# Set attention and a maxout layer: pooling in column-tiled form, paced loads, and another order in the head

## The chip, the cores and the metric

The kernel runs on one core of a Trainium2 chip. The metric is the device time of one execution in microseconds (us). TensorE (PE) multiplies, VectorE (DVE) and ScalarE (ACT) take results out of the eight PSUM banks, GpSimd (POOL) issues loads and adds in on-chip memory, and SyncE (SP) issues output stores and transposing transfers.

## The reference

For each of four batches b, x[b] is 12544 x 128 and the 32 inducing points I are 32 x 128:

```python
def mab(q, kv):
    s = scale * (q @ kv.transpose(0, 2, 1))
    s = s - s.max(-1, keepdims=True)
    a = np.exp(s)
    a /= a.sum(-1, keepdims=True) + 1e-09
    return a @ kv
h = mab(I, x)          # pooling: 32 points look at all of x
a = mab(x, h)          # every row of x looks at the 32 points
h1 = a @ w1; h2 = a @ w2           # 128 -> 1024
out = np.maximum(h1, h2) @ w_out   # 1024 -> 128
```

So h of a batch needs the whole of that batch, and only then can rows of the output be made.

## The kernel before, in words

A batch is 98 chunks of 128 rows. A chunk holds every 98th row, so that a transfer is contiguous for each partition. x lives in on-chip memory twice: as loaded (tiles xn, seven or eight parts of up to 14 chunks, twelve slots that all batches share) and transposed (xT, one tile for even and one for odd batches). Batch 0 is transposed by PE in the head of the kernel (L233, L237, L240); batches 1 to 3 by transposing transfers that SP issues (L168).

Pooling of a part, before: p1_scores multiplies each chunk of xT by the inducing points, 14 products of 32 columns (L249), and ACT takes the exponential into et (L258). p1_accum multiplies each chunk of xn by et and sums 14 products in PSUM (L292). VectorE adds the result into hacc (L303), and GpSimd adds et into eacc (L305). At the end of a batch GpSimd folds eacc (small_fold, L310 and L311), small_h sums it over partitions with fp32 products by ones (L339), takes the reciprocal (L343) and makes hT, h transposed and repeated four times (L346). small_hwd makes h(w2 - w1) (L371), small_m1 makes h w1 w_out (L392).

The maxout is computed as max(h1, h2) = h1 + relu(h2 - h1). So a group of chunks needs: a stage (L479), the scores of four quarters of chunks against h in column-tiled form, with an exponential on ACT (L491) into e; phases (L827), four row-tiled products at a time, one for each quarter, each filling a PSUM bank that ACT (L843) or VectorE (L846) turns into relu; finals (L652), products of 128 columns by w_out that sum over the 1024 inner columns; dens (L519, L529) for the softmax denominators; and an eviction by VectorE (L692) that multiplies by the reciprocals, after which SP stores (L717). The part h1 goes in as a linear term, a product by m1, within a phase.

TensorE knows three modes here: full (one 128 x 128 array), row (four arrays of 32 rows) and col (four of 32 columns). Phases are in row mode, stages in col mode, the rest in full mode.

The order of instructions is fixed when the program is written out. A class Clock estimates when each engine and bank will be free, and a loop chooses at each step: a phase, if banks and data are expected ready; otherwise one final (final_one); a stage when the staged work runs low. side_work puts in the pooling of the next batch at due points that are counted in chunks done, and only when the modelled data are ready:

```python
p_first, p_step = (16, 5) if b == 1 else (0, 7)
for i in range(7):
    s = int(p_first + p_step * i)
    at(base + s, p1_scores, b, i)
    at(base + s + 2, p1_accum, b, i)
```

The engines run that order in their queues; each waits only for its operands and for buffers to come free. keep_busy puts products by zeros into waits that the model foresees (L630), and fill does so in the head (L537).

## Time and profile before

| | |
|---|---|
| time, median of 3 runs | 339.89 us (339.79 to 341.38) |
| profiled span | 337.8 us, TensorE clock granted 1.0 |
| DMA moved | 50.60 MB, mean 150 GB/s |
| HBM read, written | 27.80 MB, 25.69 MB |
| relu on ACT, L843 | 460 of 600 ns |
| relu on VectorE, L846 | 324 of 681 ns |
| finals on PE, L652 | 3136 |
| transposing transfers, L168 | 42, landing 3.4 us after issue |

The page names a group of instructions by its line in the code, its engine and operation, and the tiles written and read. A PE instruction's duration includes its way through the array, so that the sum of durations counts overlapping work twice; what a group of products takes from the next is the time between starts. In the first 28 us the kernel pools batch 0 as its parts arrive, and finals start at about 28.2 us. The pooling of batches 1 to 3 lies at about 46 to 82, 123 to 154 and 188 to 233 us, among phases and finals. The last 85 us and more have none.

### The profile page before, as it was taken

What the parts mean: (1) busy time and instruction counts of PE and PEld (TensorE: products, weight loads), DVE (VectorE), ACT (ScalarE), POOL (GpSimd) and SP (SyncE); (2) the same over time, 40 slices, a digit from 0 to 9 for tenths busy, and PEclk for the clock granted to TensorE, in tenths of its full rate; (3) what the DMA queues carried; (4) which work ended last, traced back from release to release, by engine and by line L of the source; (5) the groups of instructions that cost most, each with busy time, mean ns of one, the idle gap of its engine ahead of it and who ended that gap; (6) DMA issues with size and microseconds to landing.
All of it is one profiled execution on the core that took longest, in us unless ns stands there. A gap on an engine that the chain in (4) does not pass through costs nothing.

```text
span 337.8 us, 13042 instructions
## 1 busy us (share of the span) xinstructions
PE 329.2 (97%) x5636; PEld 255.4 (76%) x5636; DVE 286.8 (85%) x525; ACT 279.3 (83%) x532; POOL 45.5 (13%) x72
## 2 busy tenths in 40 slices
PE   7988999999999999999999999999999999999996
PEld 3876777777777777787777778877777777777785
DVE  2248999989988899998899989889999998898873
ACT  2558888896996998888998888887999899989961
POOL 7270002234000011144000012121000000000000
PEclk9999999999999999999999999999999999999999
DMA  7999989948985879529976679621222322231233
GB/s 127 212 255 213 199 206 183 177 133 168 244 225 156 174 144 190 135 95 177 249 211 127 156 168 201 147 78 67 103 86 97 109 95 74 88 125 66 95 126 111
DMA packets 60313, 50.60 MB, mean 150 GB/s; under 512 B 42304, under 2 KB 44768, under 8 KB 60256
## 3 DMA queue, kind: packets, MB, share of 16 engines
q1 hardware_dynamic: 54576, 35.35, 40.2%
q0 software_dynamic: 5680, 14.42, 22.0%
q8 instruction: 44, 0.72, 0.9%
q14 instruction: 13, 0.11, 0.1%
HBM read 27.80 MB, written 25.69 MB: 158 GB/s over the span
## 4 chain that ended last, share of the span: by engine, by line
PE 85%; POOL 1%; ACT 1%; DMA 1%; DVE 1%; issue 1%; SPq 0%; POOLq 0%
PE ps L652 56%; PE ps L827 21%; PE ps L479 2%; PE ps L249 2%; PE ps L292 2%; PE ps L339 1%; DMA xT<-xn 1%; PE ps L519 1%; POOL eacc L305 1%; DVE relu L846 1%; ACT relu L843 1%; POOL eacc L310 0%; PE ps L371 0%; SPq L168 0%; PE ps L630 0%
## 5 line engine op out<-in xcount | busy, mean ns | idle before, releaser
L843 ACT ACTIVATE relu<-ps 128x512 f16<-128x512 f32 x460 | 245.8, 600 | 38.2 <-PE ps L827 32.0
L846 DVE TENSOR_SCALAR relu<-ps 128x512 f16<-128x512 f32 x324 | 208.8, 681 | 20.9 <-PE ps L827 18.6
L652 PE MATMUL ps<-woutp,relu 128*128 128x128 f16 x3136 | 222.2, 220 | 0.0
L652 PEld LDWEIGHTS <-relu 128*128 128x128 f16 x3136 | 177.3, 98 | 38.4 <-issue 27.8
L827 PE MATMUL ps<-e,hwd 32*128 32x512 f16 (+2 forms) x880 | 88.6, 360 | 0.5 <-ACT e L491 0.3
L692 DVE TENSOR_TENSOR o<-ps,rp 128x512 f32<-128x512 f32 (+3 forms) x108 | 68.5, 634 | 8.3 <-PE ps L652 5.4
L827 PEld LDWEIGHTS <-hwd 32*128 32x128 f16 x880 | 24.9, 91 | 20.8 <-issue 1.1
L827 PE MATMUL ps<-m,e 32*128 32x128 f16 x381 | 38.6, 217 | 0.0
L305 POOL TENSOR_TENSOR eacc<-eacc,et 128x448 f32<-128x448 f32 x18 | 18.6, 1035 | 81.8 <-ACT et L258 81.8
L827 PEld LDWEIGHTS <-e 32*128 32x128 f16 x381 | 21.3, 92 | 2.9 <-issue 0.2
L258 ACT ACTIVATE et<-ps 128x448 f16<-128x448 f32 (+2 forms) x29 | 15.6, 538 | 3.0 <-PE ps L249 2.9
L249 PE MATMUL ps<-inducingT,xT 128*128 128x32 f16 x392 | 15.5, 177 | 1.3 <-DMA xT<-xn 0.5
L162 POOL DMA_DIRECT2D xn<-in_x_dram x29 | 15.7, 553 | 2.5 <-POOLq L960 0.8
L249 PEld LDWEIGHTS <-xT 128*128 128x128 f16 x392 | 13.1, 96 | 2.3 <-ACT xT L240 0.8
L300 POOL CAST eacc<-et 128x448 f32<-128x448 f16 x3 | 1.7, 556 | 89.9 <-ACT et L258 89.9
L237 DVE COPY xT<-ps 128x1024 f16<-128x1024 f16 (+2 forms) x8 | 5.1, 632 | 9.4 <-PE ps L233 9.4
L240 ACT COPY xT<-ps 128x768 f16<-128x768 f16 (+2 forms) x8 | 5.6, 704 | 8.9 <-PE ps L233 8.9
L491 ACT ACTIVATE e<-ps 128x512 f16<-128x512 f32 (+2 forms) x21 | 11.9, 571 | 0.0
L479 PE MATMUL ps<-xT,hT 128*32 128x512 f16 (+3 forms) x114 | 10.5, 366 | 0.1
L292 PE MATMUL ps<-et,xn 128*128 128x32 f16 x294 | 10.6, 176 | 0.0
L292 PEld LDWEIGHTS <-xn 128*128 128x128 f16 x294 | 9.7, 96 | 0.0
L233 PE MATMUL ps<-identity,xn 128*128 128x128 f16 x98 | 6.8, 219 | 0.5 <-DMA xn<-in_x_dram 0.4
(75 smaller groups left out, 100.2 us busy)
## 6 DMA issues: line engine op xcount, KB each, us to landing
out_dram<-o SPq DMA_DIRECT2D x90, 256.0 KB, 2.4
xn<-in_x_dram POOLq DMA_DIRECT2D x27, 448.0 KB, 11.2
out_dram<-o SPq DMA_DIRECT2D x10, 128.0 KB, 2.0
wf<-in_moe_w_dram POOLq DMA_DIRECT2D x4, 256.0 KB, 11.6
xT<-xn SPq DMA_TRANSPOSE x42, 3.4
out_dram<-o SPq DMA_DIRECT2D x6, 64.0 KB, 1.8
out_dram<-o SPq DMA_DIRECT2D x2, 192.0 KB, 3.2
xn<-in_x_dram POOLq DMA_DIRECT2D x1, 256.0 KB, 13.6
```

Source lines behind the costliest of these rows:

```text
L162: nc.gpsimd.dma_start(out=xn_at[b, i][:, 0:n, :], in_=xr[b, :, k0 : k0 + n, :])
L249: nc.tensor.matmul(out=ps[:, j * M : (j + 1) * M], lhsT=xT_tiles[b % 2][:, k0 + j, :], rhs=inducingT, start=True, stop=True,)
L258: nc.scalar.activation(out=et[:, 0:n, :], in_=ps[:, 0 : n * M], func=AF.Exp, scale=scale)
L292: nc.tensor.matmul(out=ps[:, 0:M], lhsT=xn[:, j, :], rhs=et[:, j, :], start=(j == 0), stop=(j == n - 1))
L305: nc.gpsimd.tensor_add(out=acc, in0=acc, in1=et)
L479: nc.tensor.matmul(out=ps[32 * q : 32 * (q + 1), 128 * t : 128 * (t + n)], lhsT=hq, rhs=xT[:, c : c + n, :], start=True, stop=True, tile_p ...
L491: nc.scalar.activation(out=blk.e2[:, 0 : 128 * wd], in_=ps[:, 0 : 128 * wd], func=AF.Exp, scale=st[0]["rs"] if blk.b == 0 else scale,)
L652: nc.tensor.matmul(out=g.ps[:, 128 * c : 128 * (c + 1)], lhsT=g.blk.relu[q][:, 128 * (jb * w4 + t) : 128 * (jb * w4 + t + 1)], rhs=woutp[: ...
L692: nc.vector.tensor_mul(osb[:, 0:n, :], g.ps[:, 0 : n * C].rearrange("p (s c) -> p s c", s=n), rp)
L827: nc.tensor.matmul(**seq[i])
L843: nc.scalar.activation(out=dst, in_=src, func=AF.Relu)
L846: nc.vector.tensor_scalar(out=dst, in0=src, scalar1=0.0, scalar2=None, op0=ALU.max)
```

## The change

Pooling of batches 1 to 3 is written anew, in units of 16 chunks (U), six to a batch (NU), with two chunks over (REST):

- pool_scores holds the inducing points as weights and streams xT through four column tiles, 512 columns each. ACT's exponential gives E, 32 points in each of four groups of partitions, and a running sum along its row (accum_out into es), so that GpSimd's adds go.
- E then has points on partitions, and the sum over x needs rows there; pool_turn has SP transpose E by a transfer. pool_accum multiplies in 16 column-tiled products of 128 columns, and VectorE adds 128 columns into hacc.
- pool_rest does the two chunks over in the old form. small_rep sums the four groups' denominators and scales hacc; small_h transposes hacc and sums the groups in one fp32 product by repd, a repeated identity.
- column_work puts this work next to phases: behind a phase, ahead of one, or together with a stage, so that mode switches are shared.
- The loads of a batch are issued after the last accumulation of the batch before it, and the first of them behind a small GpSimd copy (pace) that reads its E sums (esr).
- In the head, the second and third load go out ahead of the building of the two identities, FILL rises, one accumulation is split, the difference of the weights (w21) is shared between GpSimd and VectorE earlier, and the transposes of w1 (weights_2) come after the first phase.

The core of the diff:

```diff
-    FILL = 10
+    FILL = 24
...
 
-    def load_x(b, i):
+    def load_x(b, i, after=None):
         k0, n = parts[b][i]
+        if after is not None:
+
+            nc.gpsimd.tensor_copy(out=pace, in_=after)
         nc.gpsimd.dma_start(out=xn_at[b, i][:, 0:n, :], in_=xr[b, :, k0 : k0 + n, :])
...
         nc.sync.dma_start(ind_sb, inducing)
         load_x(0, 0)
+        load_x(0, 1)
         make_identity(nc, identity16)
-        load_x(0, 1)
+        load_x(0, 2)
         make_identity(nc, identity32)
-        for i in range(2, len(parts[0])):
+        for i in range(3, len(parts[0])):
...
+        for dst, f in ((rep32, DOWN / scale), (repd, 1.0)):
...
-        def p1_accum(b, i):
+        def p1_accum(b, i, lo=0, hi=P1):
...
+        U = 16
+        NEU = 5
+        NU = K // U
+        REST = K - U * NU
...
+        def pool_scores(b, u):
+            if u == 0:
+                st[b]["es"] = smp.tile([128, NU + 1], F32, name=f"es_{b}", tag="esu")
+                nc.gpsimd.memset(st[b]["es"], 0.0)
             bi, ps = bank([128, 512])
-            ck.wait(max(ready, ck.bank[bi]), "p1")
-            for j in range(n):
+            ck.wait(ck.bank[bi], "p1")
+            for g in range(4):
                 nc.tensor.matmul(
-                    out=ps[:, 0:M], lhsT=xn[:, j, :], rhs=et[:, j, :], start=(j == 0), stop=(j == n - 1)
+                    out=ps[32 * g : 32 * (g + 1), :],
+                    lhsT=inducingT,
+                    rhs=xT_tiles[b % 2][:, U * u + 4 * g : U * u + 4 * (g + 1), :],
+                    start=True,
+                    stop=True,
+                    tile_position=(0, 32 * g),
+                    skip_group_check=True,
                 )
-            end = ck.run(0.029 * n)
-            if i == 0:
-                st[b]["hacc"] = smp.tile([C, M], F32, name=f"hacc_{b}", tag="hacc")
-                nc.vector.tensor_copy(out=st[b]["hacc"], in_=ps[:, 0:M])
-                st[b]["eacc"] = smp.tile([128, P1, M], F32, name=f"eacc_{b}", tag="eacc")
-                nc.gpsimd.tensor_copy(out=st[b]["eacc"], in_=et)
+            end = ck.run(0.226, "col")
+            eu = etp.tile([128, 512], F16, name=f"eu_{b}_{u}", tag="eu", bufs=NEU)
+            nc.scalar.activation(
+                out=eu, in_=ps, func=AF.Exp, scale=scale, accum_out=st[b]["es"][:, u : u + 1]
+            )
+            ck.bank[bi] = ck.on_act(end, 0.65)
+            st[b]["eu", u] = eu, ck.bank[bi]
...
+        def pool_turn(b, u):
+            eT = etp.tile([128, 4, 128], F16, name=f"eT_{b}_{u}", tag="eT", bufs=NEU)
+            nc.sync.dma_start_transpose(eT, st[b]["eu", u][0].rearrange("p (j t) -> p j t", j=4))
+            st[b]["eT", u] = eT, ck.pe
+
+        def pool_accum(b, u):
+            bi, ps = bank([128, 512])
+            ck.wait(ck.bank[bi], "p1")
+            eT = st[b]["eT", u][0]
+            st[b]["sum", u] = True
+            last = u == NU - 1
+            for j in range(4):
+                for g in range(4):
+                    nc.tensor.matmul(
+                        out=ps[32 * g : 32 * (g + 1), 0:128],
+                        lhsT=eT[:, j, 32 * g : 32 * (g + 1)],
+                        rhs=xn_of(b, U * u + 4 * g + j),
+                        start=(j == 0),
+                        stop=(j == 3 and not (last and g < REST)),
+                        tile_position=(0, 32 * g),
+                        skip_group_check=True,
+                    )
+            if last:
+                et = st[b]["et"][0]
+                for g in range(REST):
+                    for rhs, lo, n in ((xn_of(b, U * NU + g), 0, 128), (ones16[:, 0:1], 128, 1)):
+                        nc.tensor.matmul(
+                            out=ps[32 * g : 32 * (g + 1), lo : lo + n],
+                            lhsT=et[:, g, :],
+                            rhs=rhs,
+                            start=False,
+                            stop=True,
+                            tile_position=(0, 32 * g),
+                            skip_group_check=True,
+                        )
+            end = ck.run(0.26, "col")
+            if u == 0:
+                st[b]["hacc"] = smp.tile([128, C], F32, name=f"hacc_{b}", tag="hacc")
+                nc.vector.tensor_copy(out=st[b]["hacc"], in_=ps[:, 0:128])
             else:
                 acc = st[b]["hacc"]
-                nc.vector.tensor_add(out=acc, in0=ps[:, 0:M], in1=acc)
-                acc = st[b]["eacc"]
-                nc.gpsimd.tensor_add(out=acc, in0=acc, in1=et)
-            ck.bank[bi] = ck.on_dve(end, 0.1)
-
-        def small_fold(b):
-            e = st[b]["eacc"]
-            nc.gpsimd.tensor_add(out=e[:, 0:7, :], in0=e[:, 0:7, :], in1=e[:, 7:14, :])
-            nc.gpsimd.tensor_add(out=e[:, 0:3, :], in0=e[:, 0:3, :], in1=e[:, 3:6, :])
+                nc.vector.tensor_add(out=acc, in0=ps[:, 0:128], in1=acc)
+            ck.bank[bi] = ck.on_dve(end, 0.2)
+            if last:
+                es = st[b]["es"]
+                nc.vector.tensor_copy(out=es[0 : 32 * REST, NU : NU + 1], in_=ps[0 : 32 * REST, 128:129])
+                esr = smp.tile([128, 1], F32, name=f"esr_{b}", tag="esr")
+                nc.vector.reduce_sum(out=esr, in_=es, axis=AX.X)
+                st[b]["esr"] = esr
+                ck.bank[bi] = st[b]["esrr"] = ck.on_dve(end, 0.2)
+                if b + 1 < B:
+                    for i in range(7):
+                        load_x(b + 1, i, esr if i == 0 else None)
...
+        def small_rep(b):
+            bi, ps = bank([128, 512])
+            ck.wait(ck.bank[bi], "p1")
+            nc.tensor.matmul(out=ps[:, 0:1], lhsT=repd, rhs=st[b]["esr"], start=True, stop=True)
+            end = ck.run(0.11)
+            rec = smp.tile([128, 1], F32, name=f"rec_{b}", tag="rec")
+            nc.vector.reciprocal(out=rec, in_=ps[:, 0:1])
+            acc = st[b]["hacc"]
+            nc.vector.tensor_scalar(out=acc, in0=acc, scalar1=rec, scalar2=None, op0=ALU.mult)
+            ck.bank[bi] = st[b]["haccr"] = ck.on_dve(end, 0.4)
...
+            nc.tensor.matmul(out=ps[:, 0:128], lhsT=st[b]["hacc"], rhs=repd, start=True, stop=True)
+            end = ck.run(0.25)
+            nc.vector.tensor_copy(out=hT4.rearrange("c q m -> c (q m)"), in_=ps[:, 0:128])
+            ck.bank[bi] = st[b]["hT4r"] = ck.on_dve(end, 0.2)
             st[b]["hT4"] = hT4.rearrange("c q m -> c (q m)")
...
+        def weights_1b(eng, sl):
+            eng.tensor_sub(w21[:, sl], w2f[:, sl], w1f[:, sl])
...
-        p1_accum(0, 5)
+        p1_accum(0, 5, 0, 8)
         p1_scores(0, 7)
+        p1_accum(0, 5, 8)
         p1_accum(0, 6)
...
+        weights_1b(nc.gpsimd, slice(768, 1024))
...
+        weights_1b(nc.vector, slice(512, 768))
+        ck.on_dve(0.0, 0.36)
...
-        nc.vector.tensor_sub(w21[:, 512:1024], w2f[:, 512:1024], w1f[:, 512:1024])
-        ck.on_dve(0.0, 0.7)
         small_hwd(0)
-        weights_2()
...
-            p_first, p_step = (16, 5) if b == 1 else (0, 7)
-            t_first, t_step = (8, 2.2) if b == 1 else (-14, 3.4)
-            for i in range(7):
-                s = int(p_first + p_step * i)
-                at(base + s, p1_scores, b, i)
-                at(base + s + 2, p1_accum, b, i)
-            end = base + int(p_first + p_step * 6)
-            at(end + 2, small_fold, b)
-            at(end + 4, small_h, b)
-            at(end + 5, small_hwd, b)
-            at(end + 6, small_m1, b)
+            t_first, t_step = (8, 2.2) if b == 1 else (-6, 3.4)
+            for u in range(NU):
+                if b == 1:
+                    s, turn, acc = 24 + 5 * u, 45 + 1.5 * u, 56 + 2 * u
+                else:
+                    s = turn = 9 + 9 * u
+                    acc = s + 10
+                at(base + int(s), pool_scores, b, u)
+                at(base + int(turn), pool_turn, b, u)
+                at(base + int(acc), pool_accum, b, u)
+            s, end = int(s), base + int(acc)
+            at(base + s + 2, pool_rest, b)
+            at(end, small_rep, b)
+            at(end, small_h, b)
+            at(end, small_hwd, b)
+            at(end, small_m1, b)
             for j in range(14):
                 at(base + int(t_first + t_step * j), transpose_x_dma, b, j)
-            if b > 1:
-                for i in range(7):
-                    at(base - 34 + 3 * i, load_x, b, i)
 
...
+            if f is pool_scores and a[1] >= NEU and ("eT", a[1] - NEU) not in d:
+                return False
+            if f is pool_turn and a[1] >= NEU and ("sum", a[1] - NEU) not in d:
+                return False
+            if f is pool_scores:
+                return d.get(("T", (U * a[1] + U - 1) // (P1 // 2)), INF) + 8.0 <= now
+            if f is pool_rest:
+                return d.get(("T", 13), INF) + 6.0 <= now
+            if f is pool_turn:
+                return d.get(("eu", a[1]), (0, INF))[1] <= now
+            if f is pool_accum:
+                return d.get(("eT", a[1]), (0, INF))[1] + 8.0 <= now and (a[1] < NU - 1 or "et" in d)
...
+        def column_work(banks):
+
+            if sorted(ck.bank)[banks - 1] > ck.pe + 0.12:
+                return False
+            if want_stage(5):
+                stage(blocks[state["stage"]])
+                state["stage"] += 1
+                return True
+            jobs = [job for job in pending if job[0] in COL and ready(*job)]
+            late = jobs and chunks_done[0] >= due[jobs[0]] + 4
+            if jobs and (ck.mode == "col" or len(jobs) > 1 or late):
+                pending.remove(jobs[0])
+                f, a = jobs[0]
+                f(*a)
+                return True
+            return False
...
         phase(plan_phase(False))
+        weights_2()
         phase(plan_phase(False))
...
+            if ck.mode != "full" and column_work(1):
+                continue
+            if min(ck.bank) <= ck.pe + 0.1 and want_stage(1):
+                stage(blocks[state["stage"]])
+                state["stage"] += 1
+                continue
...
+            early = 0.2 if ck.mode == "col" else 0.0
+            if tp < INF and lag() <= 128 + LIMIT and (tp <= ck.pe + early or tp <= tf and tf > ck.pe):
+                if column_work(len(jobs) + 1):
+                    continue
                 phase(jobs)
```

## Prediction

> **What bounds the kernel now.** I read four views in this order: the busy table of the page, stage windows, the time-ordered list of TensorE (PE) instructions, the waits.
>
> ```profile
> PE 329.2 (97%) x5636; PEld 255.4 (76%) x5636; DVE 286.8 (85%) x525; ACT 279.3 (83%) x532; POOL 45.5 (13%) x72
> ...
> L249 PE MATMUL ps<-inducingT,xT 128*128 128x32 f16 x392 | 15.5, 177 | 1.3 <-DMA xT<-xn 0.5
> L292 PE MATMUL ps<-et,xn 128*128 128x32 f16 x294 | 10.6, 176 | 0.0
> ```
>
> ```profile
> 85.00:150.00 65.00, 65.00 (x1168) 50.62 (x1166) 59.08 (x106) 57.27 (x111) 6.46 (x7) 1.00 0.74 172
> 235.00:320.00 85.00, 85.00 (x1389) 65.03 (x1389) 77.91 (x134) 78.63 (x152) 0.00 (x0) 1.00 0.26 93
> ```
>
> In the windows the columns are the stretch, its length, then busy time of PE, PE weight load, VectorE (DVE), ScalarE (ACT), GpSimd, the clock, the DMA share and GB/s. PE is busy for the whole of both, at full clock. VectorE and ScalarE reach 92% in the last stretch, which has no pooling, and PE still never waits there.
>
> A busy PE is not a PE at its peak, so I priced blocks by the time from one block's first start to the next block's.
>
> ```profile
> 56.28 0.50 PE L249 MATMUL ps<-inducingT,xT 128*128 128x32 f16 x14
> 56.63 0.72 PE L652 MATMUL ps<-woutp,relu 128*128 128x128 f16 x10
> ...
> 57.88 0.50 PE L292 MATMUL ps<-et,xn 128*128 128x32 f16 x14
> 58.23 0.33 PE L652 MATMUL ps<-woutp,relu 128*128 128x128 f16 x3
> ...
> 59.02 0.40 PE L479 MATMUL ps<-xT,hT 128*32 128x512 f16 x4
> 59.35 0.56 PE L652 MATMUL ps<-woutp,relu 128*128 128x128 f16 x7
> ...
> 75.68 0.22 PE L652 MATMUL ps<-woutp,relu 128*128 128x128 f16 x1
> 76.08 1.08 PE L339 MATMUL ps<-eacc,ones 128*128 128x32 f32 x8 [0.18 <-POOL eacc L311]
> 77.00 0.55 PE L652 MATMUL ps<-woutp,relu 128*128 128x128 f16 x7
> ```
>
> Fourteen score products take 0.35 us (56.28 to 56.63), fourteen accumulations 0.35, four column-tiled products of 512 columns (a stage) 0.33, the E sum 0.92. Over the whole trace: finals 195.7 us, phases 74.7 (220, each 0.33), stages 8.7, scores of batches 1 to 3 8.8, accumulations 7.7, E sums 2.8. The finals fit 0.056 us each plus about 0.09 ahead of each phase; no idle is left in them. So PE work taken out of batches 1 to 3 shortens the kernel unless another engine steps in.
>
> ```profile
> PEld ps L339 <- POOL eacc L311: 1.1, 3, 0.5
> ...
> PE ps L249 <- DMA xT<-xn: 0.5, 2, 0.3
> ```
>
> The reader sees the only waits of the old pooling on PE: 1.1 us for GpSimd's fold, and some for x transposes.
>
> **What the Trainium skill says.** "TensorEngine Tiling (Array Packing)", Key Properties: changing the tiling mode drains TensorE. The trace agrees: two full-mode 512-column products at L371 take 0.43 us, 0.215 each, while a stage of four concurrent ones takes 0.33; so a switch costs about 0.11. "TensorE: Matmul & The Clock Gate", Measured speedup vs the span model: tiles of different column groups run side by side, the span being one product plus 4 ns per further tile. L479 agrees (0.33 for four, not 0.86). The same tiling page, Restrictions: column tiling excludes fast weight load; no run here shows what that costs when sixteen short products follow each other. "DMA: Bandwidth & Descriptors", Anatomy of one DMA: a semaphore wait sits on the issuing sequencer. The trace agrees: the SP queue waits 161.9 us in all for evictions at its output stores, so a transpose behind a store starts late.
>
> **The change part by part.**
>
> Removed from PE: 21 score groups, 8.8 us with their waits on transposes; 21 accumulation groups, 7.7; three E sums, 2.8; the waits for GpSimd ahead of them, 1.1. Sum 20.4.
>
> Added to PE, counted in the instruction order of the two builds:
> - 18 pool_scores, each four column-tiled products of 512 columns: 0.225 x 18 = 4.1.
> - 18 pool_accum, each sixteen products of 128 columns, four at a time. If tiles overlap as at L479 that is 4 x 128 columns, 0.215; a row-tiled phase with sixteen pairs takes no longer (0.33) than one with four, so issue is no floor there. If the 32-column weight loads ran one by one at the 27 ns that a small product takes (0.11 for four at L519), it is 0.43. I take 0.25: 4.5; bounds 3.9 to 7.7.
> - Column visits rise from 27 to 46 while the phases stay 220: 19 more switches of 0.11, 2.1.
> - pool_rest, six small products, 0.15; 36 small products in the last accumulations, at 5 to 25 ns each, 0.6.
> - small_rep, one fp32 product: 0.3 like small_sums at L358, x 3 = 0.9. small_h, one fp32 product of 128 columns; one of 32 columns costs 0.23 at L339; I take 0.4 x 3 = 1.2.
> Sum 13.55, net on PE -6.9; with the upper price of pool_accum -3.7, with the lower one and cheap fp32 -8.
>
> VectorE and ScalarE: VectorE loses 21 adds and copies of 32 columns (179 ns each, 3.8) and three reciprocals and products (1.9); it gains 18 adds of 128 columns (287 ns as at L692, 5.2) and some 3.1 of small operations. Four relus move to ScalarE. ScalarE trades 21 exponentials of 551 ns (11.6) for 18 of 613 (11.0), up to 0.1 more each for the running sum, which no row shows. Together they gain about 3 us on 566, while the pooling stretches get 2 us shorter each: from 90% to about 94%, against 92% where PE was still full. The order also shows some 50 finals without a phase ahead of batch 3's first stage, where the evictions starve. I charge 1.0 us, bounds 0 and 3.
>
> GpSimd and DMA: its 21 sums and folds go (22.3 us), hidden anyway. The loads of a batch now wait behind a copy that needs the E sums; queued behind it are only loads and one memset. They come at finals of about chunk 73 and 172, where the old ones came at 64 to 82 and 162 to 180; seven loads at 2.15 us each (the spacing at which the head's parts arrive) need 15 us, and the first transposes are due some 19 chunks later, about 15 us at 0.78 us a chunk; the later parts are needed later still. No cost.
> SP gains 18 transposes of E, 60 in place of 42. Behind them stand output stores; six output buffers cover some 18 us. An x transpose takes 1.27 us to issue and 3.4 to land, up to 4.9; pool_accum is put 8 us after its issue. Hidden, if SP is not late.
>
> Head: the second load goes out about 0.5 us earlier, which I value at 0.4 for each later part. FILL adds 14 products of 0.056, 0.8, ahead of the part from which PE, not the load, sets the pace: +0.4 net. Splitting the accumulation removes waits of 0.24 and 0.16. The second half of w21 is ready before its product (0.42 waited at L371), and w1's transposes (0.54) move to where PE waits for hwd anyway, though their evacuation then queues behind relus. I take -0.8 in all, bounds -1.6 and +0.6.
>
> Sum: -6.9 - 0.8 + 1.0 = -6.7; 339.9 - 6.7 = 333.2.
>
> **The rivals.**
> (a) The evictions become the bound: PE finds no free bank in the pooling stretches, and two thirds of the gain is lost. For it: 94% in my sum and eight banks. Against it: the last stretch at 92% without a wait. About 339.9 - 2.4 = 337.5.
> (b) Weight loads in column mode do not overlap: 18 x 0.18 = 3.2 more, 336.4. For it: the exclusion of fast weight load; against it: L479's four loads start within 10 ns.
> (c) PE waits for E transposes: SP issues in order behind stores that wait for evictions, so at each of 18 accumulations PE stands for 0.5 us, 9 us in all: 333.2 + 9 = 342.2, slower than before. For it: the old kernel waited 0.24 and 0.30 us inside two score groups for just such transposes. Against it: 8 us of margin over 4.7.
>
> **How the numbers follow.** Chances: forecast (330 to 335.5) 0.60, (a) 0.12, (b) 0.13, (c) 0.09, a larger gain 0.06. The range 330.0 to 338.0 holds the forecast, (a) and (b) and leaves out (c) and the larger gain. Faster needs 338.2 or less: 0.87; within 0.5% 0.07; slower 0.06.
>
> **What would show it.** In the changed profile: pool_scores about 0.23 us and pool_accum about 0.25 from start to start without the switch; PE still at 65 of 65 us in the middle stretches; no PE wait on eT. It would be wrong if pool_accum takes over 0.4, if waits on eT or on ACT's exponentials stand in PE's list, or if the head ends later than the 28.2 us at which finals start now.

## The result and the profile after

| | before | changed |
|---|---|---|
| time, median beside each other | 340.63 us (339.79 to 342.16) | 335.07 us (334.71 to 336.63) |
| the same, measured again later | 339.74 us (339.05 to 341.45) | 334.86 us (334.57 to 341.18) |
| profiled span | 337.8 us | 334.6 us |
| PE products | 5636 | 5413 |
| transposing transfers | 42 | 60 |

The ratio is 0.984 (0.980 to 0.988), and 0.986 (0.983 to 0.988) when measured again: the changed kernel is faster by 1.4 to 1.6%, about 5 us. The forecast was 333.2 us; the time is 1.7 to 1.9 us above it and inside the range. One thing is needed to read the profiles: in many executions the granted TensorE clock falls to half for a stretch, mostly one of about 3.5 us between 24 and 36 us, which costs up to 2 us, and the profile after has it (24.6 to 28.2 us) while the one before does not.

From the page of the changed kernel, the busy table and the groups that replace the old scores and accumulations (busy time, mean ns of one, idle time ahead):

```profile
PE 324.8 (97%) x5413; PEld 245.3 (73%) x5413; DVE 284.4 (85%) x528; ACT 280.9 (84%) x554; POOL 23.4 (7%) x51
...
L328 ACT ACTIVATE eu<-ps 128x512 f16<-128x512 f32 x18 | 10.9, 619 | 0.2 <-DMA eT<-eu 0.2
...
L365 PE MATMUL ps<-xn,eT 128*32 128x128 f16 x288 | 6.6, 221 | 0.0
...
L317 PE MATMUL ps<-xT,inducingT 128*32 128x512 f16 x72 | 6.5, 385 | 0.0
...
eT<-eu SPq DMA_TRANSPOSE x18, 2.5
```

PE is still busy for 97% of the span, GpSimd went from 45.5 to 23.4 us, and neither pool_accum (L365) nor pool_scores (L317) has idle time ahead of it. The E transposes (last line) land 2.5 us after issue.

The windows of the changed kernel have the columns of those before (stretch, length, busy PE, weight load, VectorE, ScalarE, GpSimd, clock, DMA share, GB/s):

```profile
25.00:30.00 5.00, 4.49 (x56) 2.58 (x53) 3.55 (x7) 4.00 (x8) 1.38 (x4) 0.69 1.08 214
85.00:150.00 65.00, 64.95 (x1099) 48.96 (x1096) 58.24 (x109) 58.00 (x116) 4.04 (x9) 1.00 0.92 193
160.00:225.00 65.00, 64.70 (x1083) 48.46 (x1081) 59.40 (x110) 60.10 (x121) 4.00 (x9) 1.00 1.00 196
```

The first row shows the fallen clock, 0.69. In the middle stretches PE is busy for 64.95 and 64.70 of 65 us and the two eviction engines for 89 to 92%: the bound is where it was, on PE, with less work in it. (The pooling of batch 2 in the kernel before begins at 111 us in its trace, not at 123.)

PE's list of the changed kernel in order of time (start, duration, what it runs, in brackets idle time ahead):

```profile
77.88 0.39 PE L920 MATMUL ps<-e,hwd 32*128 32x512 f16 x4
78.20 0.67 PE L365 MATMUL ps<-xn,eT 128*32 128x128 f16 x32
78.80 0.68 PE L746 MATMUL ps<-woutp,relu 128*128 128x128 f16 x9
...
91.18 0.38 PE L409 MATMUL ps<-esr,repd 128*128 128x1 f32 x2
91.42 0.50 PE L746 MATMUL ps<-woutp,relu 128*128 128x128 f16 x6
...
92.51 0.44 PE L438 MATMUL ps<-repd,hacc 128*128 128x128 f32 x2
92.79 1.00 PE L746 MATMUL ps<-woutp,relu 128*128 128x128 f16 x15
...
167.72 0.35 PE L409 MATMUL ps<-esr,repd 128*128 128x1 f32 x2 [0.29 <-DVE esr L399]
167.93 0.66 PE L746 MATMUL ps<-woutp,relu 128*128 128x128 f16 x9
```

Between a phase and a group of finals stand two pool_accum, 32 products, in 0.60 us with one mode switch: some 0.245 each. small_rep (L409) takes 0.24 and 0.21, small_h (L438) 0.28. At small_rep PE waits for VectorE's sum of the denominators (L399). The waits of the changed kernel name it (total, times, longest):

```profile
PEld ps L409 <- PE ps L746: 0.6, 2, 0.4
...
PE ps L920 <- ACT relu L936: 0.5, 2, 0.3
...
PE ps L409 <- DVE esr L399: 0.3, 1, 0.3
```

The old wait for GpSimd's fold, 1.1 us, is gone; the wait for esr at small_rep put 0.9 in its place. In PE's list it shows as finals just ahead of small_rep that take longer than their number explains, by 0.22, 0.46 and 0.20 us in the three batches.

Adding up, from one start to the next, all of PE's list from the first final to PE's last product gives the balance. For the changed kernel I set beside the profile that of the experiment with wide fills, whose work after the head is the same and whose clock stayed at 1.0 in the head; they differ by no more than 0.1 us in a row.

| PE, us from start to start | before | changed | wide fills |
|---|---|---|---|
| first final starts at | 28.18 | 29.56 | 27.70 |
| finals | 198.7 | 199.4 | 199.4 |
| phases | 73.3 | 75.4 | 75.3 |
| stages | 8.0 | 7.7 | 7.7 |
| scores: old, then pool_scores | 8.7 | 5.3 | 5.3 |
| accumulations: old, then pool_accum | 7.7 | 5.1 | 5.1 |
| pool_rest and the last small products | - | 0.7 | 0.7 |
| E sum and small_h | 2.8 | 0.8 | 0.8 |
| small_rep | - | 0.7 | 0.7 |
| keep_busy | 1.5 | 0.6 | 0.6 |
| dens, hwd, both m1 rows | 6.0 | 6.0 | 6.0 |
| sum, to PE's last product | 306.6 | 301.6 | 301.6 |

So PE is shorter by 5.0 to 5.1 us after the head, the head by 0.5 where the clock holds, and the tail from PE's last product to the end of the span is some 0.3 longer.

### The profile page after: what moved, and what is told of

Same layout as the page of the kernel before. It is cut to its first block, busy times and chain, and to the rows that moved or that the text cites. A ratio compares the mean times of both kernels' runs of the same rounds, so it can differ in the third digit from the quotient of the medians.

```text
span 334.6 us, 12612 instructions
## 1 busy us (share of the span) xinstructions
PE 324.8 (97%) x5413; PEld 245.3 (73%) x5413; DVE 284.4 (85%) x528; ACT 280.9 (84%) x554; POOL 23.4 (7%) x51
## 4 chain that ended last, share of the span: by engine, by line
PE 87%; DVE 4%; DMA 3%; issue 2%; ACT 1%; POOL 1%; POOLq 0%; DVEq 0%
PE ps L746 57%; PE ps L920 21%; DMA xn<-in_x_dram 3%; PE ps L572 2%; DVE relu L939 2%; PE ps L365 1%; PE ps L317 1%; ACT relu L936 1%; PE ps L240 1%; DVE o L786 1%; PE ps L612 1%; POOL xn L165 1%; PE ps L461 1%; PE ps L278 0%; ACT xT L247 0%
## 5 line engine op out<-in xcount | busy, mean ns | idle before, releaser
L939 DVE TENSOR_SCALAR relu<-ps 128x512 f16<-128x512 f32 x320 | 205.6, 681 | 22.5 <-PE ps L920 20.9
L746 PE MATMUL ps<-woutp,relu 128*128 128x128 f16 x3136 | 217.9, 220 | 0.1
L920 PE MATMUL ps<-e,hwd 32*128 32x512 f16 (+2 forms) x880 | 89.7, 361 | 1.0 <-ACT relu L936 0.5
L244 DVE COPY xT<-ps 128x1024 f16<-128x1024 f16 (+2 forms) x8 | 5.1, 634 | 10.4 <-PE ps L240 10.4
L328 ACT ACTIVATE eu<-ps 128x512 f16<-128x512 f32 x18 | 10.9, 619 | 0.2 <-DMA eT<-eu 0.2
L164 POOL COPY pace<-esr 128x1 f32<-128x1 f32 x2 | 0.4, 183 | 137.0 <-DVE esr L399 137.0
L572 PEld LDWEIGHTS <-hT 128*32 128x32 f16 x114 | 3.1, 92 | 5.4 <-issue 4.4
L622 DVE RECIPROCAL rp<-ps 128x16 f32<-128x16 f32 (+2 forms) x28 | 6.7, 238 | 0.0
L365 PE MATMUL ps<-xn,eT 128*32 128x128 f16 x288 | 6.6, 221 | 0.0
L612 PE MATMUL ps<-ones_q,e 128*128 128x4 f16 x102 | 6.6, 165 | 0.0
L317 PE MATMUL ps<-xT,inducingT 128*32 128x512 f16 x72 | 6.5, 385 | 0.0
```

The source lines that it names most:

```text
L328: nc.scalar.activation(out=eu, in_=ps, func=AF.Exp, scale=scale, accum_out=st[b]["es"][:, u : u + 1])
L365: nc.tensor.matmul(out=ps[32 * g : 32 * (g + 1), 0:128], lhsT=eT[:, j, 32 * g : 32 * (g + 1)], rhs=xn_of(b, U * u + 4 * g + j), start=(j = ...
L572: nc.tensor.matmul(out=ps[32 * q : 32 * (q + 1), 128 * t : 128 * (t + n)], lhsT=hq, rhs=xT[:, c : c + n, :], start=True, stop=True, tile_p ...
L612: nc.tensor.matmul(out=ps[:, 4 * t : 4 * t + 4], lhsT=blk.e2[:, 128 * t : 128 * (t + 1)], rhs=ones_q, start=True, stop=True,)
L746: nc.tensor.matmul(out=g.ps[:, 128 * c : 128 * (c + 1)], lhsT=g.blk.relu[q][:, 128 * (jb * w4 + t) : 128 * (jb * w4 + t + 1)], rhs=woutp[: ...
L920: nc.tensor.matmul(**seq[i])
```

## The experiments

Each was timed beside the kernel before, and ratios are to it. Lines that start with - are the changed kernel's, except where said.

**The two halves of the change alone.** First the changed pooling with the old head:

```diff
-    FILL = 24
+    FILL = 10
...
-        load_x(0, 1)
         make_identity(nc, identity16)
-        load_x(0, 2)
+        load_x(0, 1)
...
-        p1_accum(0, 5, 0, 8)
+        p1_accum(0, 5)
         p1_scores(0, 7)
-        p1_accum(0, 5, 8)
...
-        weights_1b(nc.gpsimd, slice(768, 1024))
...
-        weights_1b(nc.vector, slice(512, 768))
...
+        weights_1b(nc.vector, slice(512, 1024))
         small_hwd(0)
+        weights_2()
...
         phase(plan_phase(False))
-        weights_2()
```

> The changed kernel with the head of before (FILL 10, the old order of the loads, one whole accumulation of part 5, the second half of w21 by VectorE behind rw, w1's transposes ahead of the first phase). Theory: the gain is PE work taken out of batches 1 to 3, about 7 us less; the new head, which starts its finals at 29.6 us in the profile against 28.2 before, gives nothing. Then this kernel takes 333 to 334.5 us, at or below the changed kernel's 335.1, and its finals start at about 28.2 us. Rival: part of the gain is the new head, as the prediction had it (0.8 us); then it takes 336 us or more.

Then the kernel before with the new head, the reverse of this diff:

> The kernel before with the head of the change alone and the old pooling. Theory: about the time of before, 340 to 341.5 us, and up to 1.5 us slower in an execution where the clock falls near 24 us. Rival (the head brings its share of the gain): 338.5 to 339.5 us.

Pooling alone: 337.43 us, ratio 0.990 (0.987 to 0.993). The head alone: 340.60 us, ratio 0.9995 (0.997 to 1.002), so nothing that can be measured, although its trace has finals start at 27.79 in place of 28.18.

The expectation for pooling alone, 333 to 334.5 us, was missed, and 337.43 lies where the rival had put it. Much of that is the clock: its mean was 0.995 or less in seven of the eight executions. In the one where it held, the time is 335.76 us, 4.0 below the ten such executions of the kernel before (median 339.76) and 0.7 to 1.2 above those of the changed kernel on two other occasions (334.57 to 335.11). So about four fifths of the gain comes from the pooling. The rest appears only where the new head stands together with the new pooling. From the first final on, pooling alone takes PE as long as the changed kernel (301.8 us); its span of 333.6 us in the execution where the clock held, less the 305.1 us that its profile has from the first final to the end, puts the first final at about 28.5 us, an estimate, against 27.70 with wide fills. This rest is read from one execution, and why the head alone gains nothing stays open.

**Fills in the head.** The changed profile had a gap of 1.03 us ahead of one product of batch 0, with the releaser "issue" (PE waited for nothing that the profile shows), and I suspected the 24 narrow fills queued before it.

```diff
-                fill(FILL)
+                bi, ps = bank([128, 512])
+                for _ in range(FILL // 4):
+                    nc.tensor.matmul(out=ps, lhsT=warm[:, 0:128], rhs=warm, start=True, stop=True)
+                ck.run(0.056 * FILL)
```

> The changed kernel with the 24 fill products of 128 columns written as 6 products of 512 columns: the same PE time, 36 PE instructions fewer in the head. Theory A: the 1.03 us that PE stands idle at 22.6 us, waiting for nothing that the profile shows, is the arrival of its instructions, so that it goes or moves with the number of instructions ahead of it; then the clock does not fall and the time is 333.3 to 334.8 us in every execution. Theory B: it depends on the data or on the fill's time; then the gap stays at the same product and the time stays at 334.7 to 336.6 us.

```diff
-    FILL = 24
+    FILL = 10
```

> The changed kernel with FILL back at 10, nothing else. If the 14 products stand in PE's way, as the prediction counted (0.8 us less what the earlier loads give back), 0.4 to 0.8 us less than the changed kernel without the fall of the clock: 334.0 us. If they only fill a wait for the load, no difference: 334.7 us. If they keep the clock up, the fall of the clock comes more often and the time is 336 us or more.

PE's list of the changed kernel at that product:

```profile
22.22 0.36 PE L278 MATMUL ps<-et,xn 128*128 128x32 f16 x8
...
23.65 0.32 PE L278 MATMUL ps<-et,xn 128*128 128x32 f16 x6 [1.03 <-issue]
```

With wide fills the same product starts 0.27 us after the one ahead of it, not 1.43. Wide fills: 334.57 us, ratio 0.985 (0.979 to 0.990). FILL at 10: 334.62, ratio 0.982 (0.978 to 0.987). Both ratios agree with that of the changed kernel within their intervals. So the 14 added fills, which the prediction priced at 0.4 net, cost nothing that can be measured: in the changed profile PE still stands 0.27 us for a load right behind them, at 16.33 us. The gap isn't explained by narrow fills either. Three kernels with 24 narrow fills show it (1.03, 0.70 and 0.44 us) and four others with the same fills do not. Nor does the fall of the clock go with it: in FILL at 10 the clock fell to 0.53 without the gap, and with wide fills it fell in one of four executions (336.77 us), where the theory had it fall in none. What makes the clock fall there stays open.

**PE's work and weight loads.** All sixteen products of pool_accum twice; the second pass starts the sum anew, so h stays what it was and only PE has more to do.

```diff
-            for j in range(4):
+            for again, j in [(r, j) for r in range(2) for j in range(4)]:
...
-                        stop=(j == 3 and not (last and g < REST)),
+                        stop=(j == 3 and not (again and last and g < REST)),
...
-            end = ck.run(0.26, "col")
+            end = ck.run(0.49, "col")
```

> The changed kernel with the sixteen products of every pool_accum issued twice, the second pass starting the sum anew: 288 column-tiled products of 128 columns more, and no other work. Theory: PE is the bound and sixteen of them take 0.23 us, so 18 x 0.23 = 4.1 us more, 338.8 to 339.5 us. If their weight loads ran one by one (0.43 us), 7.7 us more, 342.8. Rival: the evictions are the bound in the pooling stretches; then under 1.5 us more, below 336.6.

PE's list of this kernel:

```profile
84.67 0.39 PE L920 MATMUL ps<-e,hwd 32*128 32x512 f16 x4
84.99 1.97 PE L365 MATMUL ps<-xn,eT 128*32 128x128 f16 x128
86.79 0.22 PE L378 MATMUL ps<-xn,et 128*32 128x128 f16 x2
```

128 products from 84.99 to 86.79 are 0.225 us for sixteen. The time is 338.43 us, ratio 0.994 (0.992 to 0.996): 3.4 us over the changed kernel for 3.9 us more of L365 in PE's list. The planner was told of the longer time and wrote 486 mode switches in place of 490, which at some 0.09 us each (the next experiment) is most of the difference. Two things follow. Column-tiled products of 128 columns run at the rate of the overlap, so the weight loads do not run one by one. And nearly the whole of an addition to PE comes out in the time, so no other engine hides it: where these products stand, PE is the bound, not the evictions.

**What it is worth to stand next to phases.** The pooling products go in from full mode, in visits of their own; the share with a stage or phase is cut out:

```diff
-                if f in COL or not ready(f, a):
+                if not ready(f, a):
                     continue
-                if f in FULL:
+                if f in FULL + COL:
...
-            jobs = [job for job in pending if job[0] in COL and ready(*job)]
+            jobs = []
```

> The changed kernel with pool_scores and pool_accum issued one at a time out of full mode, as the old pooling was, and only stages left next to phases: 63 column visits in place of 46 and 531 mode switches in place of 490. Theory: 41 switches of about 0.11 us on PE, 4.5 us more, 339 to 340 us. Rival: switches hide behind PE's waits for weights; then under 1.5 us more.

In the written order, visits to col mode rise from 46 to 63 and mode switches from 490 to 531. PE's list of this kernel, at a place where its clock is at 1.0:

```profile
90.03 0.40 PE L746 MATMUL ps<-woutp,relu 128*128 128x128 f16 x4
90.36 0.41 PE L365 MATMUL ps<-xn,eT 128*32 128x128 f16 x16
90.70 0.56 PE L746 MATMUL ps<-woutp,relu 128*128 128x128 f16 x7
```

A pool_accum between finals takes 0.34 us, against 0.245 for each of the two that shared a visit. The time is 338.59 us, ratio 0.994 (0.992 to 0.996): 3.5 us over the changed kernel, 0.09 for each of 41 switches, a little below the 0.11 read from the old profile. So placing the work next to phases is worth some 3 of the 5 us; the column-tiled form in visits of its own gains only 2. The order around these visits is another too, and its part was not measured apart.

**The load wait.** The copy that holds the loads back is taken out. GpSimd then no longer waits for the E sums, and each load goes out as soon as its slot is free. The written order of the other engines stays the same.

```diff
-                        load_x(b + 1, i, esr if i == 0 else None)
+                        load_x(b + 1, i)
```

> The changed kernel without GpSimd's copy that reads the E sums: the loads of the next batch then go out as soon as their slots are free, five of those of batch 2 right behind batch 1's, at about 26 us. Theory (the prediction costed the wait at nothing): the same within 0.5 us, 334.5 to 335.6 us. Rival: the early loads slow the transposes of x for batch 1, whose margin is 8 us, and PE waits for xT or eT; then 1 to 5 us more, and xT transposes landing well over 4.2 us.

The result missed that by far: 352.33 us, ratio 1.032 (1.026 to 1.039), 17 us slower than the changed kernel and 12 slower than the one before. The waits of this kernel within 55 to 105 us, and then PE's list in that stretch:

```profile
PE ps L365 <- DMA eT<-eu: 8.2, 1, 8.2
...
PE ps L317 <- DMA xT<-xn: 4.3, 4, 2.7
```

```profile
60.67 0.38 PE L317 MATMUL ps<-xT,inducingT 128*32 128x512 f16 x1 [1.00 <-DMA xT<-xn]
...
63.76 1.34 PE L317 MATMUL ps<-xT,inducingT 128*32 128x512 f16 x4 [2.71 <-DMA xT<-xn]
...
94.91 0.41 PE L365 MATMUL ps<-xn,eT 128*32 128x128 f16 x16
103.50 0.62 PE L365 MATMUL ps<-xn,eT 128*32 128x128 f16 x16 [8.19 <-DMA eT<-eu]
```

PE stands first for x transposes, then 8 us for one E transpose. What the trace says of the E transposes of this kernel, and then of the changed one:

```profile
DMA to landing us min/median/max: 2.3/2.8/16.9
```

```profile
DMA to landing us min/median/max: 2.3/2.5/4.4
```

And of the x transposes, in this kernel and then in the changed one:

```profile
DMA to landing us min/median/max: 2.9/3.4/14.0
```

```profile
DMA to landing us min/median/max: 2.9/4.2/7.4
```

When loads run beside the transposes, single transposes land 14.0 us (x) and 16.9 us (E) after issue. The slow E transpose is issued at 86.52 us and lands at 103.47; loads issued at 85.01 to 95.60 are under way all that time. These waits are not the whole of the 17 us. PE's waits for transposes in this stretch add up to 12.5, and in and behind them the clock falls:

```profile
62.00:69.00 7.00, 5.12 (x44) 3.79 (x45) 1.61 (x3) 1.28 (x3) 0.00 (x0) 0.51 0.95 221
103.50:110.00 6.50, 6.50 (x75) 5.32 (x76) 3.49 (x10) 2.09 (x5) 1.06 (x2) 0.51 1.04 242
```

At a clock of 0.51 the 11.6 us that PE is busy here would have taken some 6 at full clock, so the fall costs about 5.7 us, an estimate. With the waits that makes 18 us, as much as this profile is longer than the changed kernel (351.4 against 332.7 to 333.1 us).

The Trainium skill, "DMA: Bandwidth & Descriptors", Anatomy of one DMA, says that a wait sits on the issuing sequencer. The trace agrees: in the changed kernel the copy stands on GpSimd for 137.0 us in its two waits, and the loads queued behind it are held back for as long. That is its purpose. From the groups of the changed kernel:

```profile
L164 POOL COPY pace<-esr 128x1 f32<-128x1 f32 x2 | 0.4, 183 | 137.0 <-DVE esr L399 137.0
```

The kernel before had no such copy, but GpSimd issued its loads in order among its adds for E, and these stood 81.8 us in 18 waits for ACT's exponentials. The change takes those adds away, and with them this pacing; the copy puts one back. That the old adds did this is read from the order and the waits; a kernel before without them was not tried.

**Releasing the loads by the last x transpose instead.** The loads move to transpose_x_dma, behind its last call for a batch:

```diff
         st[b]["T", j] = ck.pe
+        if j == 13 and 0 < b < B - 1:
+            for n_ in range(7):
+                load_x(b + 1, n_, xT_tiles[b % 2][:, K - 1, 0:1] if n_ == 0 else None)
...
-                if b + 1 < B:
-                    for i in range(7):
-                        load_x(b + 1, i, esr if i == 0 else None)
```

> The changed kernel with the next batch's loads let go by the last transpose of x of the batch at hand in place of its E sums, some 20 us earlier. If only the transposes of x must be kept clear of loads, the 7 us at xT of the unpaced kernel go, and its wait at eT as well: 335 us. If the transposes of E need the quiet too, one wait at eT of about 8 us stays: 341 to 345 us.

376.10 us, ratio 1.107 (1.103 to 1.111), but it is no answer to the question. In the written order these loads stand ahead of accumulations of the older batch that read the same slots, so in the last batches those accumulations wait for, and sum, the next batch's rows: part of the pooling is changed. The waits of this kernel:

```profile
PE ps L368 <- DMA xn<-in_x_dram: 36.8, 3, 20.9
```

The 36.8 us are that wait. Whether a release earlier than the E sums would do is left open.

**More and less work for ScalarE.** First each pool exponential twice, the second into a spare tile, with the longer time told to the planner; then half of each E left out, as zeros written by GpSimd, so that half of the rows do not count in h:

```diff
-            ck.bank[bi] = ck.on_act(end, 0.65)
+            spare = etp.tile([128, 512], F16, name=f"spare_{b}_{u}", tag="spare", bufs=1)
+            nc.scalar.activation(out=spare, in_=ps, func=AF.Exp, scale=scale)
+            ck.bank[bi] = ck.on_act(end, 1.25)
```

> The changed kernel with the exponential of every pool_scores done twice, the second time into a spare tile, which the written order is told of: 18 x 0.62 = 11.2 us more on ACT and no more on PE. Theory: ACT and VectorE have slack enough in the pooling stretches, so under 1.5 us more, 335 to 336.5 us. Rival: the evictions are the bound; the 11 us are shared by the two engines, 5 us more, 340 us.

```diff
+            nc.gpsimd.memset(eu[:, 256:512], 0.0)
             nc.scalar.activation(
-                out=eu, in_=ps, func=AF.Exp, scale=scale, accum_out=st[b]["es"][:, u : u + 1]
+                out=eu[:, 0:256], in_=ps[:, 0:256], func=AF.Exp, scale=scale, accum_out=st[b]["es"][:, u : u + 1]
             )
-            ck.bank[bi] = ck.on_act(end, 0.65)
+            ck.bank[bi] = ck.on_act(end, 0.43)
```

> The changed kernel with ACT's exponential in pool_scores over 256 of the 512 columns, the rest set to zero by GpSimd: half of E is left out, so ACT has 18 x about 0.22 = 4 us less, and the written order is told. After exp_twice (9 us more for 11 us of ACT) theory A: the evictions are as near to being the bound as PE is, and the time falls by 2 us or more, to 333 us or below. Theory B: PE alone is the bound of the changed kernel, and ACT hurts only when it gets more; then 334.3 to 335.2 us.

Twice: 349.57 us (343.85 to 352.37), at least 9 us over the changed kernel. Half: 343.22 us, ratio 1.011 (1.008 to 1.014), so slower too, with less to do. Both missed, and both are confounded: the planner reads the duration, so the written order changed as well. PE's list of the kernel with the exponentials twice, at its end:

```profile
334.11 0.39 PE L922 MATMUL ps<-e,hwd 32*128 32x512 f16 x1
335.19 0.40 PE L748 MATMUL ps<-woutp,relu 128*128 128x128 f16 x4 [0.69 <-ACT relu L938]
335.52 0.38 PE L922 MATMUL ps<-e,hwd 32*128 32x512 f16 x1
336.59 0.40 PE L748 MATMUL ps<-woutp,relu 128*128 128x128 f16 x4 [0.69 <-ACT relu L938]
```

Two phases of a single product are left over and cost 1.07 us each; the kernel with half of E has two such phases at its end too, and the changed order has none. With half of E, PE also waited 2.0 us for an E transpose, and the zeros put GpSimd's queue, which issues the loads, behind E transposes for 76.5 us. So these two runs say how much the written order matters, and not whether the evictions take part of the gain. The same order with another load on ScalarE was not tried.

**A smaller step between the pooling units.** Ahead of batch 3's first stage some 50 finals pass without a phase. With wide fills, and units 7 chunks apart instead of 9, that gap goes:

```diff
-                    s = turn = 9 + 9 * u
+                    s = turn = 9 + 7 * u
```

> The changed kernel with the wide fill (6 products of 512 columns) and the pooling of batches 2 and 3 spaced 7 chunks apart in place of 9, so that h of batch 3 is ready before the staged work runs out; in the changed kernel 50 finals pass there without a phase and phases then wait 0.8 us. If that gap is lost time: 333.3 to 334.0 us. If it is made up elsewhere: 334.5 us. If the transposes of E then come too close to those of x and PE waits for them: 336 us or more.

335.59 us, ratio 0.988 (0.986 to 0.990): 1.0 us above wide fills alone, and 0.7 above the changed kernel measured on that occasion. The intervals of the ratios overlap, but all six executions (335.31 to 337.0 us) lie above all five of the changed kernel whose clock held (334.57 to 335.11), so it is a little slower. The waits of this kernel:

```profile
PE ps L339 <- DMA xT<-xn: 2.0, 2, 1.1
```

The gap ahead of the stage is gone, but the scores of the two chunks over (L339) now come before the last x transposes have landed, and PE stands 2.0 us for them. No version was found that is clearly faster than the changed kernel.

**The changed kernel again**, beside the last of these:

> The changed kernel itself, for a ratio taken beside the runs that follow. 334.7 to 335.1 us where the clock stays up; ratio to before 0.984 to 0.986.

334.86 us, ratio 0.986 (0.983 to 0.988), as in the table above. The profile is that of its longest execution (341.18 us), with the clock at half from 24.0 to 30.8 and from 34.2 to 41.2 us. It shows one thing that the first profile of this kernel does not have:

```profile
217.76 0.41 PE L365 MATMUL ps<-xn,eT 128*32 128x128 f16 x16 [1.46 <-DMA eT<-eu]
```

PE stands 1.46 us for an E transpose.

## Why the prediction was right, and where it was off

**PE is the bound.** Right. Products added in the doubled accumulation come out in the time (3.4 of 3.9 us), and the middle stretches of the changed profile have PE busy for 64.7 to 65 of 65 us. One reading differs: finals of the kernel before add up to 198.7 us in the list, where the prediction has 195.7, but no term of its sum uses that figure.

**Removed, 20.4.** The products are gone as counted: 8.72 + 7.74 + 2.84 = 19.3. The 1.1 for the fold wait was not gained: the E sums now come from VectorE, and PE waits 0.9 for them at small_rep. The prediction counted the wait taken away and no wait in its place.

**Added, 13.55.** The rows that answer to it are 5.33 + 5.12 + 0.71 + 0.83 + 0.67 = 12.7, less 0.3 because stages now share visits: 12.3. The fp32 products were priced too high, 0.4 for small_h where it took 0.28 and 0.3 for small_rep where it took 0.21 to 0.24, and pool_accum at 0.25 was right. The 36 small products in the last accumulations are 12 in the trace, 0.47 us with 0.6 charged. This error and the one in the part removed cancel, which is luck: with the waits, -19.3 + 12.3 - 0.2 = -7.2 against -6.9.

**Weight loads in column mode (rival b).** Refuted: 0.225 us for sixteen. The Trainium skill, "TensorEngine Tiling (Array Packing)", Restrictions and Gotchas, excludes fast weight load there; the doubled products show no cost of that with weights of 32 columns. The overlap agrees with "TensorE: Matmul & The Clock Gate", Measured speedup vs the span model.

**The head, -0.8.** -0.5 where the clock holds (28.18 to 27.70), nothing that the head alone could show in its time, and some 0.9 on top of the new pooling, from one execution. FILL, charged at +0.4 net, is free as far as the runs can tell. The prediction took a head that ends later than 28.2 us as a sign of being wrong; the profile after has that, at 29.56, with the clock fallen.

**Evictions and starved phases, 1.0.** This is the term that was mis-sized, though inside its bounds of 0 and 3. With the parts above taken out, 5.1 less after the head in place of 7.2 leaves 2.1 us. In the balance it is 2.1 more for the same 220 phases and 0.7 more for finals, of which the waits at small_rep replace those at the fold, less 0.9 of keep_busy. By place it comes apart in three. In the first 8 us after the first final the phases take 1.2 us longer and keep_busy 1.2 less: the same time under another name, since PE waits there, 0.5 us of it by name for ScalarE's relu (the waits above), where the kernel before ran products by zeros. Net, 0.2 us are lost there. Some 0.8 stands in one place of the changed kernel's PE list:

```profile
253.60 0.39 PE L920 MATMUL ps<-e,hwd 32*128 32x512 f16 x2
...
254.14 0.40 PE L572 MATMUL ps<-xT,hT 128*32 128x512 f16 x4
254.47 0.40 PE L746 MATMUL ps<-woutp,relu 128*128 128x128 f16 x4
254.70 0.33 PE L724 MATMUL ps<-warm 128*128 128x128 f16 x3
254.97 0.74 PE L920 MATMUL ps<-e,hwd 32*128 32x512 f16 x10
255.64 1.01 PE L746 MATMUL ps<-woutp,relu 128*128 128x128 f16 x15
```

The phase that starts at 253.60 lasts to 254.14, 0.54 for 0.33; keep_busy takes 0.27; the next phase takes 0.67. Just before lie the 50 finals without a phase, for which nothing was left to evict. The prediction saw them in the written order and took 1.0 for all of this, where it is 2.1. The remaining 1.1 us is spread over finals and phases, and no run says what it is. The load on the evictions did not grow by more than was priced: VectorE and ScalarE are busy for 565.3 us in all, against 566.1 before, where the prediction added 3, and in the fullest stretch (160 to 225 us) ScalarE rises from 57.38 to 60.10 of 65 us, to 92.5% where the prediction had 94.

**ScalarE's running sum, "up to 0.1 more".** Right. The groups of the changed kernel have it as an instruction of its own with a duration of 226 ns, 4.1 us in all:

```profile
L328 ACT ACTIVATION_READ_ACCUMULATOR eu<-ps 128x1 f32 x18 | 4.1, 226 | 0.0
...
L393 DVE TENSOR_TENSOR hacc<-ps,hacc 128x128 f32<-128x128 f32 x15 | 4.3, 285 | 0.6
```

But durations on ScalarE overlap, as on PE, and what counts is the time between starts. ScalarE's list of the changed kernel:

```profile
61.08 0.62 ACT L328 ACTIVATE eu<-ps 128x512 f16<-128x512 f32 x1
61.56 0.23 ACT L328 ACTIVATION_READ_ACCUMULATOR eu<-ps 128x1 f32 x1
61.65 0.63 ACT L328 ACTIVATE eu<-ps 128x512 f16<-128x512 f32 x1
```

The read starts 0.48 us after the exponential, and the next instruction 0.09 after the read, so the sum adds 0.09 us to each of 18, 1.7 in all. VectorE's add of 128 columns is as priced, 285 ns for 287.

**The evictions as the bound (rival a).** Not as stated: it would have lost two thirds of the gain, and a PE that pays 3.4 for 3.9 us is not waiting for banks. Whether a weaker form of it is in the 1.1 us that stay unexplained is open, since the two runs on ScalarE didn't decide it.

**PE waits for E transposes (rival c).** Not at the size it had: the first profile of the changed kernel has no wait of PE on eT, the second has a single one of 1.46 us, in the execution of 341.18 us. So the sign "no PE wait on eT" held in one profile of two. The mechanism is real: without the copy it makes the kernel slower than before. So the reason I gave for "no cost" of the load wait, that the loads have time enough, was true and missed what the wait does; I had priced what it might delay and not what it keeps apart.

The sum, with wide fills for the changed kernel and two decimals: -7.16 on PE, +2.09 for phases and finals, -0.48 for the head, +0.34 for the tail, -5.21. The spans differ by 337.8 - 332.6 = 5.2 us, the times of the changed kernel by 4.9 to 5.6.

## What to carry to other kernels

When one engine is the bound and its list has no idle time, price a change by the time from start to start of its blocks, mode switches included: here the visits saved were worth at least as much as the products. When a change takes work off an engine that issues loads in order, ask what that work was pacing, and put a wait in its place: without it, transposes that stand beside loads can land many microseconds late. And when a plan is written out from a model, an experiment that tells the model a new duration also tests another order. Last, a duration in the profile is not a price where instructions overlap: read the time from start to start on every engine.

## What the hardware showed that was not expected

- The accumulated sum of an exponential is a separate read with a duration of 226 ns beside the 619 ns of the exponential itself, but adds only 0.09 us from start to start (0.57 in place of 0.48).
- Sixteen column-tiled products of 128 columns, each with its own weight load, took 0.225 us, 14 ns each.
- Transposing transfers that took 2.5 (E) and 4.2 us (x) in the median landed up to 16.9 and 14.0 us after issue beside bulk loads.
- The granted TensorE clock fell to half for about 3.5 us, or twice for about 7, between 24 and 42 us in several profiles: in the changed kernel's behind a PE gap of 1.03 us, in that of FILL at 10 (24.0 to 27.6 us) with no gap over 0.24 us in the 15 us before. In the kernel without the copy it fell for 7.0 and 10.4 us, from within waits of 2.7 and 8.2 us on.
